# The last 64 rows of q and k loaded four tokens to a partition, batch 1 by SyncE's queue, channel weights issued sooner, the second gather's copies planned later

## The chip, the cores and the metric

The kernel runs on one core of a Trainium2 chip. The metric is the time of one execution on the device in microseconds (us). The engines go by the profile's names: PE is TensorE's matmul and PEld its weight load, DVE is VectorE, ACT is ScalarE, POOL is GpSimd, SP is SyncE. SP and ACT issue loads on hardware queues, POOL on a software queue.

## The reference

For 8 batches of 8 heads, 576 tokens and 64 values a head: attention in which a token sees the 32 tokens to either side, and 8 global tokens see and are seen by all. The result, heads side by side, is the input x (8 x 576 x 512) of a mixer block: one pair of matmuls over tokens, one over channels, each with a residual.

```python
mask = np.abs(pos[:, None] - pos[None, :]) <= window      # window = 32
mask = mask | is_global[:, None] | is_global[None, :]
scores = np.where(mask, scale * (q @ kT), -1e9)
attn = softmax(scores) @ v
...
h = np.maximum(xt @ w_tok1, 0.0) @ w_tok2                 # 576 -> 256 -> 576
u = x + h.transpose(0, 2, 1)
h2 = np.maximum(u @ w_ch1, 0.0) @ w_ch2                   # 512 -> 1536 -> 512
return u + h2
```

The eight global positions are an input, so which columns are global is known only on the chip.

## The kernel before

**Tiles.** All tiles are allotted once. A batch's q and k come as f32 into `lq` and `lk` (128 partitions, 8 heads, four tokens side by side in a partition, 64 values): `load_qk` (L504) thus loads the first 512 tokens in runs of 1 KB. The last 64 rows (`S - LAST` to `S`) of q and of k go into the two halves of one tile, `lr` (L60): `load_rest` (L513) puts one token into a partition, so a run is 64 values, 256 bytes. v goes by tokens into `lv` (`load_v`, L521). `cast_qk` and `cast_v` copy them to f16 (`qk`, `rn`, `vsh`). There is one copy of `lq`, `lk`, `lr`, `lv`, `qk` and `rn`: a batch's load waits for the casts of the batch before.

**Turning.** q and k are needed with the 64 values on the partitions. For batches 0 to 2 PE turns them (`turn_pe` L562, `rest_pe` L583, which turns `rn`), and copies bring them into `qT` and `kT`; from batch 3 on DMA transposes on SP do it (`turn_dma` L639). The copies undo the order of four tokens to a partition.

**Global columns.** For batch 0 `glob_pe` (L594) picks the global tokens out of `qk` and `rn` by matmuls with a one-hot right-hand side `ohq` (L359, made in `f_ohq` L378): for each pair of heads and for q and k, four products for the first 512 tokens and one for the last 64. For the other batches indirect DMAs (`f_gather` L486, on POOL) fetch the rows, the first gather for batches 1 to 3, the second for 4 to 7; `glob_rows` (L616) copies them to f16 (L619) and PE turns them (L623).

**The rest of a batch.** `scores` (L660: matmuls L675, exponential on ACT L685, mask on DVE L691), `glob_keys` (L698), `glob_sums` (L717, matmul L722), `values` (L733, matmuls L742 and L755, division L782 and L783), `token1` (L799), `token2` (L817), `turn_u` (L842), `chan1` (L864, matmul L868, 128x512 each), `chan2` (L889, matmul L911) and the store (L922). In the first 34 us PE also runs matmuls on zeros into free banks (`warm`, L284; their tile is `zt`).

**Order.** The kernel schedules itself when it is built. Every piece of work is entered by `op` (L96) with the engines that may do it and a cost on each, a priority, what it reads and writes, and for a DMA the tuple `dma`: transfer time, weight of its queue against others, time to landing, and number of pieces. `run` (L119) then simulates the engines and the queues, and at each step gives out the piece that could start first; so each engine gets a fixed order of instructions. On the chip an engine works through its order and waits where something is not there yet. `late` adds to the time at which the planner takes a transfer as landed, as does `LATE` (L116) after 36 us. `behind` lets a piece be issued only after another one on the queue. `slot` (L168) gives out the eight banks of PSUM.

**Queues.** For batch 0 SP issues `lr`, `lq`, `lk` and `lv` (L941 to L945). POOL fills constants (`f_pads`, `f_pads2`), then a `gate` (L934, a copy of one column of a tile that a load fills) makes it wait for batch 0's second piece of v, and behind that it issues `w1`, `w1l`, `w2`, the first gather's k half, batch 1's `lr`, `lq` and `lk`, the three thirds of the first channel weights (`f_wc1`, L475) and of the second (`f_wc2`, L481), batch 1's v and batch 2's loads. Loads of batch 3 and later are issued by SP (q, k, rest) and ACT (v), paced by `paced` (L914).

## Time and profile before

| What | Value |
|---|---|
| median of 3 runs | 307.86 us (306.68 to 311.13) |
| profiled execution, device time | 308.4 us |
| its span, first to last instruction | 306.7 us |
| busy, PE / PEld | 289.9 us (95%) / 154.9 us (51%) |
| busy, DVE / ACT / POOL | 187.3 us (61%) / 178.9 us (58%) / 60.2 us (20%) |
| instructions | 7290, of them 2955 matmuls |
| mean granted clock of TensorE | 0.987 |
| moved by DMA | 51.31 MB in 94820 packets, 73730 of them under 512 bytes |

A row of the order of time reads: start, duration, engine (with a q: its queue issuing), line, operation, output <- inputs, shapes, count, and in brackets how long the engine had stood idle and for whom. In a table by stretches each engine has its busy time and its number of instructions, then come the granted clock, the busy share of the DMA engines and GB/s. A row of a group has after the bar its busy time in us and the mean of one in ns. Matmuls overlap: the 128x512 matmul of the first channel stage takes 380 ns by its own row, and eight of them behind one another take 1.89 us.

### The profile page before, as it was taken

The numbers are of one execution on the slowest core, as the hardware profiler recorded it, in microseconds if no ns is written. First come the engines' busy times: TensorE is split into PE (matmuls) and PEld (weight loads), VectorE is DVE, ScalarE is ACT, GpSimd is POOL, SyncE is SP. The second block draws the span as 40 slices with busy tenths as digits, with TensorE's granted clock in tenths as the row PEclk, the third lists the DMA queues.
The fourth block names the chain that finished last, engine by engine and source line by source line (L and its number), as shares of the span: only waits on it lengthen the run. The fifth ranks groups of instructions, "written<-read, shape, count | busy, mean of one in ns | idle before, by whom it ended". The sixth has DMA issues, their size and how long they took to land. (4 is left out here: it accounts for less than half of the span.)

```text
span 306.7 us, 7290 instructions
## 1 busy us (share of the span) xinstructions
PE 289.9 (95%) x2955; PEld 154.9 (51%) x2955; DVE 187.3 (61%) x411; ACT 178.9 (58%) x325; POOL 60.2 (20%) x109
## 2 busy tenths in 40 slices
PE   5969989997999989999989999999999999999995
PEld 3746645444474444544456445444555445444643
DVE  7778866668786536994476655976587357230012
ACT  3873895376986369812996089714992183305600
POOL 8489635642001010002000100002000200020000
PEclk9798999999999999999999999999999999999999
DMA  6988999999997973499946995699844411071013
GB/s 170 257 137 272 220 226 212 298 214 301 193 149 139 309 205 62 96 163 230 311 76 131 218 338 143 98 214 220 288 100 90 135 38 37 8 148 69 0 71 104
DMA packets 94820, 51.31 MB, mean 167 GB/s; under 512 B 73730, under 2 KB 90242, under 8 KB 94786
## 3 DMA queue, kind: packets, MB, share of 16 engines
q1 hardware_dynamic: 62480, 26.36, 39.9%
q0 software_dynamic: 8704, 18.45, 24.1%
q10 hardware_dynamic: 23602, 6.03, 11.1%
q8 instruction: 23, 0.38, 0.5%
q14 instruction: 11, 0.09, 0.1%
HBM read 36.11 MB, written 9.44 MB: 149 GB/s over the span
## 5 line engine op out<-in xcount | busy, mean ns | idle before, releaser
L868 PE MATMUL bank<-uT,wc 128*128 128x512 f16 x384 | 92.3, 380 | 2.5 <-DVE qT L591 1.7
L911 PE MATMUL bank<-wc,b 128*128 128x512 f16 x384 | 87.5, 379 | 0.0
L685 ACT ACTIVATE e<-bank 128x648 f16<-128x648 f32 x64 | 42.9, 740 | 44.3 <-PE bank L675 43.2
L860 ACT ACTIVATE b<-bank 128x512 f16<-128x512 f32 x87 | 51.6, 620 | 26.3 <-PE bank L868 26.2
L911 PEld LDWEIGHTS <-b 128*128 128x128 f16 x384 | 36.8, 98 | 42.6
L868 PEld LDWEIGHTS <-wc 128*128 128x128 f16 x384 | 35.1, 98 | 43.5 <-issue 4.3
L922 POOL DMA_DIRECT2D out_dram<-osb x28 | 15.6, 556 | 198.6 <-DVE osb L919 198.6
L919 DVE TENSOR_TENSOR osb<-u,bank 128x512 f32<-128x512 f16 x32 | 21.9, 686 | 46.3 <-PE bank L911 46.1
L691 DVE TENSOR_TENSOR e<-e,masku 128x1296 f16<-128x1296 f16 x28 | 23.3, 832 | 20.5 <-ACT e L685 20.1
L548 ACT CAST vsh<-lv 128x512 f16<-128x512 f32 (+3 forms) x44 | 26.6, 621 | 7.5 <-DMA lv<-in_v_dram 7.1
L836 DVE TENSOR_TENSOR u<-x,bank 128x512 f16<-128x512 f16 x30 | 18.7, 682 | 8.1 <-PE bank L823 7.8
L783 DVE TENSOR_TENSOR x<-bank,rr 128x512 f16<-128x512 f32 x32 | 22.1, 692 | 1.1
L823 PE MATMUL bank<-a,w 128*128 128x512 f16 x80 | 19.9, 379 | 0.6 <-DVE a L811 0.4
L675 PEld LDWEIGHTS <-kT 64*128 64x128 f16 x576 | 11.3, 96 | 15.2 <-issue 14.1
L805 PE MATMUL bank<-x,w 128*128 128x512 f16 x64 | 18.7, 379 | 0.0
L536 ACT CAST qk<-lk 128x512 f16<-128x512 f32 x27 | 16.6, 627 | 1.7 <-DMA lk<-in_k_dram 1.7
L742 PE MATMUL bank<-rf,lf 128*64 128x264 f16 x144 | 16.1, 294 | 1.2 <-ACT b L860 0.9
L675 PE MATMUL bank<-qT,kT 64*128 64x72 f16 x576 | 15.6, 196 | 1.2 <-ACT e L685 1.2
L536 ACT CAST qk<-lq 128x512 f16<-128x512 f32 x26 | 15.8, 624 | 1.2 <-DMA lq<-in_q_dram 0.7
L755 PEld LDWEIGHTS <-e 128*64 128x64 f16 x576 | 16.1, 115 | 0.1
L755 PE MATMUL bank<-vsh,e 128*64 128x66 f16 x320 | 15.9, 198 | 0.0
L653 DVE COPY kT<-raw 128x512 f16<-128x512 f16 x20 | 12.0, 599 | 5.2 <-DMA raw<-qk 4.9
(166 smaller groups left out, 333.8 us busy)
## 6 DMA issues: line engine op xcount, KB each, us to landing
out_dram<-osb POOLq DMA_DIRECT2D x28, 256.0 KB, 4.3
lq<-in_q_dram SPq DMA_DIRECT2D x11, 512.0 KB, 7.0
lk<-in_k_dram SPq DMA_DIRECT2D x11, 512.0 KB, 9.2
lv<-in_v_dram ACTq DMA_DIRECT2D x15, 256.0 KB, 5.4
wc<-in_moe_w_ch_dram POOLq DMA_DIRECT2D x6, 512.0 KB, 13.3
lq<-in_q_dram POOLq DMA_DIRECT2D x4, 512.0 KB, 8.5
lk<-in_k_dram POOLq DMA_DIRECT2D x4, 512.0 KB, 9.8
lv<-in_v_dram ACTq DMA_DIRECT2D x10, 192.0 KB, 5.7
```

The source lines that it names most:

```text
L536: COPY[e](out=qk[:, ti, p].rearrange("q i (r d) -> q r i d", r=2), in_=(lq, lk)[ti][:, hs])
L548: COPY[e](out=vsh[i][a:z, c, :, 0:D], in_=lv[a:z, c])
L675: nc.tensor.matmul(ps_tile[keys[z]][:, u // 3, UW * (u % 3) : UW * (u % 3) + UW], lhsT=kT[r, 64 * u : 64 * u + P], rhs=qT[r, u // 2, UW * ...
L685: op([("A", 0.595)], pri + 1, lambda e, par=par: nc.scalar.activation(out=es[i][:, 2 * p + par].rearrange("p (n u) x -> p n u x", n=3), in ...
L691: op([("V", 0.85)], pri + 2, lambda e: nc.vector.tensor_mul(out=e2, in0=e2, in1=masku.unsqueeze(1).to_broadcast([P, 2, NB, UW])), r=["mask ...
L755: nc.tensor.matmul(o[:, VW * hh : VW * hh + VW], lhsT=es[i][:, h, 2 * tau + c, x : x + 64], rhs=vod[i][:, tau, h, :] if c else vsh[i][:, t ...
L783: nc.vector.tensor_tensor(out=xo, in0=pq[:, :, :, 0:D], in1=rr.unsqueeze(3).to_broadcast([P, 2, NP, D]), op=ALU.mult,)
L823: nc.tensor.matmul(ps_tile[key], lhsT=w2[:, ch, P * tau - sh : P * tau - sh + P], rhs=a1[:, ch, :], start=(ch == 0), stop=(ch == 1 and not ...
L860: nc.scalar.activation(out=out, in_=in_, func=AF.Relu)
L868: nc.tensor.matmul(ps_tile[key], lhsT=wc1[:, cc, P * j : P * j + P], rhs=uT[:, cc, :], start=(cc == 0), stop=(cc == 3))
L911: nc.tensor.matmul(ps_tile[key], lhsT=w, rhs=wc2[:, j, :], start=(j == 0), stop=(j == NJ - 1))
L919: nc.vector.tensor_add(out=osb, in0=uls[b // 2 % 2] if last else u16s[i][:, tau], in1=ps_tile[key])
```

## The change

- `lr` is laid out as [128, 2, 256]: four tokens side by side in a partition, 16 partitions to a head, two heads per group of partitions (index r). `load_rest` becomes four loads (q and k, r = 0 and 1) in runs of 1 KB, for batch 0 on ACT's queue (`"K"`) instead of SP's.
- `rn` holds the same in f16 with another order, and the copies after the turn (`rest_pe`, `turn_dma`) undo it.
- `glob_pe` needs four products for the last rows, with a one-hot `ohr` that also picks the pair of heads (`f_ohr`), eight matmuls for each sum instead of five. `ohq` gets eight columns of positions instead of six.
- Batch 1's `lr`, `lq` and `lk` are issued by SP behind batch 0's v, not by POOL.
- On POOL batch 1's constants are filled early, a second gate waits for batch 1's third load of q and k, and behind it come the first channel weights, then the second ones and batch 1's v as before. Batch 2's loads and the second gather stand behind these. Fills of `w1l` and `w2` move to `f_pads2`.
- The second gather's copies (`late` 12.0 instead of 0) are planned later.
- The planner's figures: `LATE` 1.5 instead of 2.0, a far larger weight for POOL's queue (`BIG`), dearer v loads on POOL, a lower weight for stores, the cost of changing the kind of matmul only when it changes from `"n"`, and dearer last pieces of `values`.

```diff
-    lr = const.tile([P, H, D], F32, name="lr")
+    lr = const.tile([P, 2, 4 * D], F32, name="lr")
...
-    RING, LATE = 4096, 2.0
+    RING, LATE = 4096, 1.5
...
-                    if e == "P" and o["mode"] != mode:
+                    if e == "P" and mode == "n" != o["mode"]:
                         c = c + 0.095
...
-    op_i = const.tile([P, NT + 1], I32)
+    op_i = const.tile([P, 8], I32)
     nc.gpsimd.iota(op_i[:, 0:4], pattern=[[1, 4]], base=0, channel_multiplier=4)
-    nc.gpsimd.iota(op_i[:, 4:5], pattern=[[1, 1]], base=S - LAST, channel_multiplier=1)
-    nc.gpsimd.iota(op_i[0:LAST, 5:6], pattern=[[1, 1]], base=S, channel_multiplier=1)
-    nc.gpsimd.iota(op_i[LAST:P, 5:6], pattern=[[1, 1]], base=S - LAST, channel_multiplier=1)
+    nc.gpsimd.iota(op_i[:, 4:8], pattern=[[1, 4]], base=S - LAST, channel_multiplier=0)
...
+    pm64 = const.tile([P, 1], F32)
+    nc.vector.tensor_scalar(out=pm64, in0=pm16, scalar1=4.0, scalar2=None, op0=ALU.mult)
+    nc.vector.tensor_scalar(out=op_f[:, 4:8], in0=op_f[:, 4:8], scalar1=pm64, scalar2=None, op0=ALU.add)
...
+    def f_ohr(e):
+        nc.vector.tensor_tensor(
+            out=ohr, in0=ohq[:, 4:8].unsqueeze(1).to_broadcast([P, 2 * NP, 4, NG]),
+            in1=blk.unsqueeze(2).unsqueeze(3).to_broadcast([P, 2 * NP, 4, NG]), op=ALU.mult,
+        )
...
+    op([("V", 0.35)], -186.5, f_ohr, r=["ohq"], w=["ohr"])
...
-    TURN, STORE = (0.75, 256, 0.35, 544), (0.78, 2048, 0.8, 128)
+    TURN, STORE, BIG = (0.75, 256, 0.35, 544), (0.78, 600, 0.8, 128), 100000
...
     def load_rest(b, pri, opts, after=(), late=0.0, ):
         for t, ten in enumerate((q, k)):
-            def f(e, t=t, ten=ten):
-                ENG[e].dma_start(
-                    out=lr[LAST * t : LAST * t + LAST], in_=ten[b, :, S - LAST : S, :].rearrange("h p d -> p h d")
-                )
+            for r in range(2):
+                def f(e, t=t, r=r, ten=ten):
+                    ENG[e].dma_start(
+                        out=lr[LAST * t : LAST * t + LAST, r],
+                        in_=ten[b, :, S - LAST : S, :].rearrange("(p r) (g i) d -> p r g (i d)", r=2, i=4)[:, r],
+                    )
...
-                COPY[e](out=rn.rearrange("p n (r d) -> p (n r) d", r=2), in_=lr)
+                COPY[e](out=rn.rearrange("p i (r d) -> p r i d", r=2), in_=lr.rearrange("p r (i d) -> p r i d", i=4))
...
-            out=kTs[i][:, :, WIN + 512 : WIN + S], in_=ps_tile[key][:, :, LAST:P]), ps=[key], w=[("kTr", i)])
+            out=kTs[i][:, :, WIN + 512 : WIN + S].rearrange("q p (g i) -> q p g i", i=4),
+            in_=ps_tile[key][:, :, LAST:P].rearrange("q i (p g) -> q p g i", p=NP)), ps=[key], w=[("kTr", i)])
...
-                    for t in range(NT):
+                    for t in range(8):
                         nc.tensor.matmul(
-                            pg[:, ti * n + p - pp.start, :], lhsT=qk[:, ti, p, t] if t < 4 else rn[:, p],
-                            rhs=ohq[:, t if t < 4 else 4 + ti, :], start=(t == 0), stop=(t == NT - 1),
+                            pg[:, ti * n + p - pp.start, :], lhsT=qk[:, ti, p, t] if t < 4 else rn[:, t - 4],
+                            rhs=ohq[:, t, :] if t < 4 else ohr[:, NP * ti + p, t - 4, :], start=(t == 0), stop=(t == 7),
                         )
...
-            load_rest(0, -196, [("S", 0.65)])
+            load_rest(0, -196, [("K", 0.5)])
...
-            if b == 1:
-                pl = -173.9
-            load_rest(b, pl, [("G", 0.73)], [n0] if b == 1 else ())
+            load_rest(b, pl if b > 1 else -179, [("G", 0.73) if b > 1 else ("S", 0.6)], [n0] if b > 1 else ())
...
-                    load_qk(b, ti, slice(h, h + 4), pl + 1 + h / 2 if b > 1 else pl + 0.1 + h / 100, [("G", 0.88)], [n0] if b == 1 else ())
+                    load_qk(b, ti, slice(h, h + 4), pl + 1 + h / 2 if b > 1 else -178 + h / 100, [("G", 0.88) if b > 1 else ("S", 0.9)], [n0] if b > 1 else ())
+            if b == 1:
+                gate(-173.5, [("l", 0, 2)], [lq[:, 4, 0, 0:1]])
...
-            op([("G", 0.77)], -173, f_wc1(0), w=[("wc1", 0)], dma=(2.6, 4096, 2.0, 512), behind=[n0])
-            op([("G", 1.0)], -174.5, f_w2, w=["w2"], dma=(2.4, 4096, 2.0, 512), behind=[n0])
-            for t in (1, 2):
-                op([("G", 0.77)], -173 + t, f_wc1(t), w=[("wc1", t)], dma=(2.6, 4096, 2.0, 512), behind=[n0])
+            op([("G", 0.9)], -174.5, f_w2, w=["w2"], dma=(2.4, BIG, 2.0, 512), behind=[n0])
...
-            op([("G", 1.2)], -18, lambda e: qk_pads(1, nc.gpsimd), w=[("qT", 1, p) for p in range(NP)] + [("kT", 1, p) for p in range(NP)] + [("qTr", 1), ("kTr", 1)], behind=[n1])
+            op([("G", 1.2)], -173.9, lambda e: qk_pads(1, nc.gpsimd), w=[("qT", 1, p) for p in range(NP)] + [("kT", 1, p) for p in range(NP)] + [("qTr", 1), ("kTr", 1)], behind=[n2])
...
-                op([("G", 2.7)], (-115 if ti == 0 else -174.2) if b == 0 else 70, f_gather(b, ti), r=["idx"], w=[("g32", b, ti)], dma=(0.1, 256, 1.7, 256), late=0.0 if b or ti else 2.3,
-                   behind=[] if b == 0 and ti == 0 else [n2])
+                op([("G", 2.7)], (-115 if ti == 0 else -174.2) if b == 0 else 70, f_gather(b, ti), r=["idx"], w=[("g32", b, ti)], dma=(0.1, 128, 1.7, 256), late=12.0 if b else (0.0 if ti else 2.3),
+                   behind=[nw] if b else [n2] if ti else [])
...
-            loads(1, n0)
-            op([("G", 0.77)], -40, f_wc2(0), w=[("wc2", 0)], dma=(2.6, 4096, 2.0, 512), behind=[len(ops) - 1])
+            loads(1)
+            n0 = len(ops) - 1
+            for t in range(3):
+                op([("G", 0.77)], -173 + t, f_wc1(t), w=[("wc1", t)], dma=(2.6, BIG, 2.0, 512), behind=[n0])
+            op([("G", 0.77)], -40, f_wc2(0), w=[("wc2", 0)], dma=(2.6, BIG, 2.0, 512), behind=[len(ops) - 1])
...
+            nw = len(ops) - 1
```

53 lines of the change are left out of this document (29 added, 24 removed).

## The prediction

> **What bounds the kernel now.** I read the head of the page first, then the busy time by stretches, then the warm-up matmuls alone (they read and write nothing that counts), then the order of time around each idle stretch of PE.
>
> ```profile
> span 306.7 us, 7290 instructions
> ```
>
> ```profile
> core 0: us, PE busy (x) PEld busy (x) DVE busy (x) ACT busy (x) POOL busy (x), PEclk, DMA share, GB/s
> 0.00:7.00 7.00, 3.61 (x16) 2.03 (x16) 5.24 (x33) 2.15 (x4) 5.82 (x27) 1.00 0.59 161
> 7.00:22.00 15.00, 12.31 (x213) 8.55 (x215) 11.22 (x37) 13.01 (x25) 9.95 (x18) 0.89 1.07 208
> 22.00:35.00 13.00, 12.49 (x168) 9.14 (x165) 11.54 (x29) 6.37 (x13) 11.60 (x18) 0.87 0.94 244
> 35.00:60.00 25.00, 23.42 (x280) 12.03 (x278) 16.82 (x34) 16.85 (x31) 13.91 (x19) 1.00 1.14 241
> ...
> 69.00:76.00 7.00, 5.09 (x65) 3.33 (x63) 5.84 (x11) 4.42 (x10) 1.71 (x3) 1.00 1.50 320
> 76.00:300.00 224.00, 221.33 (x2153) 113.37 (x2153) 130.02 (x258) 129.43 (x235) 13.27 (x24) 1.00 0.66 147
> 300.00:306.70 6.70, 2.94 (x26) 2.28 (x24) 1.53 (x3) 0.00 (x0) 0.00 (x0) 0.90 0.37 119
> ```
>
> ```profile
> 0.00:7.00 7.00, 3.56 (x15) 1.93 (x15) 0.27 (x1) 0.21 (x1) 1.00 0.59 161
> 7.00:22.00 15.00, 2.39 (x13) 1.14 (x13) 0.00 (x0) 0.00 (x0) 0.89 1.07 208
> 22.00:35.00 13.00, 1.20 (x8) 0.74 (x8) 0.00 (x0) 0.00 (x0) 0.87 0.94 244
> ```
>
> The reader is to see that TensorE (PE) sets the time, and that only the first quarter has something to give. From 76 to 300 us PE is idle for 2.67 of 224 us. Before that it is idle for 3.39, 2.69, 0.51, 1.58 and 1.91 us in the five stretches shown, 10.1 us in all, and 7.15 us of its busy time up to 35 us are warm-ups (3.56, 2.39, 1.20). So about 17 us before 76 us hold no work. The end (300 to 306.7) is not touched by the change. The profiled execution took 308.4 us, 1.7 more than its span; the median of the runs is 307.86. I make the sum against 308.4, which stands 0.2% above that median.
>
> **Part 1, the start: the last rows leave SyncE's queue.**
>
> ```profile
> 0.82 0.77 SPq L516 DMA_DIRECT2D lr<-in_q_dram  x1
> 1.25 0.52 ACTq L445 DMA_DIRECT2D gidx_r<-in_global_idx_dram  x1
> 2.30 0.62 SPq L506 DMA_DIRECT2D lq<-in_q_dram  x1
> 6.34 0.62 ACT L533 CAST rn<-lr 128x512 f16<-128x512 f32 x1 [4.03 <-DMA lr<-in_k_dram]
> 6.87 0.61 ACT L536 CAST qk<-lq 128x512 f16<-128x512 f32 x1
> ```
>
> SP issues two `lr` loads first, so batch 0's first `lq` goes out at 2.30. The change puts `lr` behind the index load on ScalarE's queue, and `lq` can go at 0.82, 1.48 us sooner; its cast at 6.87 was behind the `rn` cast, which waited for `lr` until 6.34. The four new issues cost 4 x 0.52 = 2.1 us on ACT after 1.77, under its 4.03 us wait. Bounds: a gain of 1.5 if all follows `lq`, a loss of 0.5 if `rn` comes later (its last issue at 1.77 + 3 x 0.52 = 3.3 instead of 0.82 + 0.77 = 1.6, some of it made good by smaller and fewer pieces) and ACT takes it first. I take a gain of 1.0, nearer to `lq`.
>
> **Part 2, three more matmuls for each global sum.** A position's column now needs four products for the last rows instead of one: 8 sums x 3 = 24 matmuls. Nothing in the trace has the new right-hand side; the nearest rows:
>
> ```profile
> 9.07 0.29 PE L601 MATMUL bank<-ohq,qk 128*128 128x8 f16 x4
> L408 DVE TENSOR_TENSOR masku<-band,rowh 128x256 f16<-128x256 f16 x1 | 0.4, 417 | 0.0
> L656 DVE COPY qT<-raw 128x512 f16<-128x512 f16 x20 | 11.7, 600 | 0.5 <-DMA raw<-qk 0.3
> L648 DVE COPY qT<-rawr 128x256 f16<-128x256 f16 x5 | 1.1, 225 | 0.7 <-DMA rawr<-rn 0.7
> ```
>
> Four take 0.29 us, at most 0.07 each, so 24 take up to 1.7 us, all inside 7 to 22 us, where PE has 2.69 us idle and 2.39 us of warm-ups as cover. The new one-hot (`f_ohr`, 256 elements: 0.42 us) and two small vector operations go into DVE's chain ahead of the first scores. Bounds 0 and 1.7 lost; I take 0.2, since ACT (13.01 of 15 us) and not PE paces that stretch. The copies of the turned last rows become strided: 600 ns for 512 elements strided (L656) is 300 for 256, against 225 (L648), so some 75 ns in 10 copies, 0.8 us of DVE, and DVE is idle 94 of the 224 us there: nothing. From batch 1 on a batch has four `lr` issues instead of two, two more at about 0.62 us (the row at 2.30); they run a batch ahead of their use, so nothing again, and 1.2 us a batch if that lead were gone.
>
> **Part 3, batch 1's q and k go by SyncE's queue, and the channel weights move up in POOL's.**
>
> ```profile
> 17.00:23.00 6.00, 4.22 (x104) 2.78 (x105) 4.57 (x14) 4.29 (x9) 5.39 (x8) 0.92 0.89 123
> 6.00:9.00 3.00, 1.72 (x19) 1.47 (x20) 2.63 (x11) 2.66 (x6) 2.44 (x7) 0.90 0.93 292
> ```
>
> ```profile
> 6.28 8.74 SPq L525 DMA_DIRECT2D lv<-in_v_dram  x5
> 23.09 0.84 POOL L506 DMA_DIRECT2D lq<-in_q_dram  x1
> 28.54 0.60 ACT L809 ACTIVATE a<-bank 128x512 f16<-128x512 f32 x1 [2.48 <-PE bank L805]
> 31.00 0.42 DVE L536 CAST qk<-lk 128x512 f16<-128x512 f32 x1
> 33.24 1.06 PE L568 MATMUL bank<-ident,qk 128*128 128x128 f16 x16
> 33.82 0.60 ACT L852 COPY uT<-bank 128x512 f16<-128x512 f16 x1
> 34.48 1.05 PE L568 MATMUL bank<-ident,qk 128*128 128x128 f16 x16
> 35.37 1.89 PE L868 MATMUL bank<-uT,wc 128*128 128x512 f16 x8
> ```
>
> Now SP is done at 15.0 and stands still, while POOL issues batch 1's q and k from 23.09. After the change they stand behind batch 0's v on SP, at about 14. By then 17 to 23 us moves only 123 GB/s, against 292 in 6 to 9, so batch 1's q and k (2 x 8 x 576 x 64 x 4 bytes, 2.4 MB) fit in some 8 us: I estimate the third load, for which the new gate on POOL waits, landed at 23 to 26 us. What that buys: ACT, which sits 2.48 us idle before 28.54, can cast batch 1 there; DVE loses casts like the one at 31.00 out of the chain that makes `u`; and the 32 transposes (33.24 and 34.48, 2.1 us) no longer stand between the last `uT` copy, done at 34.42, and the first channel matmul at 35.37. I take 0.95 for that gap and 1.15 for two to three casts fewer in the chain ahead: 2.1. Bounds: 0 if ACT's room comes at the wrong time, 3.3 if the transposes and the warm-ups of that stretch (2.1 + 1.2) all go.
>
> That needs the weights too:
>
> ```profile
> L476 POOL DMA_DIRECT2D wc<-in_moe_w_ch_dram x1: 829/829/829, 26.1 to 26.1; - x1
> ...
> DMA to landing us min/median/max: 8.9/8.9/8.9
> ```
>
> ```profile
> 49.68 0.62 ACT L548 CAST vsh<-lv 96x512 f16<-96x512 f32 x1 [0.67 <-DMA lv<-in_v_dram]
> 50.35 0.24 PE L722 MATMUL bank<-vsh,eg 128*32 128x132 f16 x4 [0.25 <-ACT vsh L548]
> ```
>
> The first third of the channel weights is issued at 26.1 and lands at 35.0, 0.4 before its first use: today no earlier start was possible. In the changed order it is issued behind the gate, at 24 to 27, but the 2.4 MB ahead of it in POOL's queue are gone, so I expect it at 29 to 31. Batch 1's v comes behind it; its last piece holds PE at 50.35 today. Of the 1.58 us that PE idles in 35 to 60, I take 0.9 as gained (bounds 0 and 1.6). Everything on POOL waits behind the gate: all channel weights, batch 1's v, batch 2's loads and the second gather. Batch 1's fills of constants are moved ahead of it, into the time that POOL waits anyway.
>
> By the Trainium skill ("DMA: Bandwidth & Descriptors", section "Issuing engines are not separate DMA queues") loads issued from different engines share the same 16 DMA engines, and another issuer saves only its issue time. By that alone this part would be worth nothing; its result is rival 2, and the 123 GB/s speak against it.
>
> **Part 4, the second gather's copies.**
>
> ```profile
> 69.73 0.23 DVE L619 CAST g_q<-g_q 128x128 f16<-128x128 f32 x1 [2.16 <-DMA g_q<-in_q_dram,idx_i]
> 71.85 0.30 ACT L619 CAST g_k<-g_k 128x128 f16<-128x128 f32 x1 [2.33 <-DMA g_k<-in_k_dram,idx_i]
> 73.34 1.02 PE L868 MATMUL bank<-uT,wc 128*128 128x512 f16 x4 [1.73 <-DVE qT L591]
> L623 PE MATMUL bank<-ident,g_q x2: 219/219/219, 26.3 to 130.1; 128*128 128x128 f16 x2
> ```
>
> DVE and ACT each stand over 2 us in front of a gather that the planner thought landed; the copies that free PE's bank are queued behind, and PE idles 1.73 us. The second gather's result is used first at 130.1. Planned 12 us later, the copies wait for nothing. Next late is batch 2's own data. I take 1.6 (bounds 0 and 1.9, all the idle time from 69 to 76).
>
> **Part 5, the planner's other figures** (landing margins, POOL's share, the cost of changing kind of matmul) do no work; they reorder. In 76 to 300 that can win at most part of 2.67 us; bounds a gain of 1.0 and a loss of 1.5; I take 0.
>
> **Sum.** 1.0 - 0.2 + 2.1 + 0.9 + 1.6 = 5.4; 308.4 - 5.4 = **303.0 us**. Its own range, by about half of each bound, is 300.5 to 306.
>
> **The rivals.** *1, more than the sum:* two stretches before 35 us run at a lower granted clock: 0.89 over 15 us and 0.87 over 13 us, 1.65 + 1.69 = 3.3 us of clock not granted. If batch 1's work fills the holes, the second stretch need not come, and if Part 3 also reaches 3.3 and the start 1.5: 303.0 - 1.7 - 1.2 - 0.5 = 299.6. For it: eight warm-ups in that stretch are there to be replaced. Against: the values of batch 0 stay a chain of short steps. The Trainium skill ("TensorE: Matmul & The Clock Gate", Part 1) says that an idle window of about 3.4 us brings half clock, on a window that runs free of the kernel; where it falls is then partly chance, and no single trace here shows that. Chance 0.26.
>
> *2, the transfers are hidden anyway:* the DMA engines are shared, and batch 1 comes no sooner than now, because w1, w2 and the gathers take the room from 17 to 23. Then Part 3 falls away, and 1.0 - 0.2 + 1.6 = 2.4 remain: 306.0. For it: DMA share 0.89 in that stretch. Against: 123 GB/s beside it. Chance 0.19.
>
> *3, slower:* the gate on POOL. It waits for a load that stands behind batch 0's v and behind the last casts of batch 0's q and k (one buffer). The first channel weights then land about 5 us after it opens (0.83 to issue, and about 4.6 by the `lq` load that was issued at 2.30 and cast at 6.87). The point where it decides is 30 us: later than that, they land after today's 35.0, and PE has little else. If it opens at 36, they land at 41, and PE loses 6 us there, gives back 1 of it, and keeps Part 4 and the start: 308.4 + 5 - 2.4 = 311.0. Against: it needs a delay of 10 us over my estimate. Chance 0.06.
>
> *4, the change does not do what it says in Part 4:* later planning only shifts the wait to another transfer, such as batch 2's v; 1.6 falls away, 304.6. Chance 0.07, inside the forecast's own range. The forecast itself: 0.42.
>
> **How the numbers follow.** Two per cent, about what a measurement of this kernel tells from no change, is 301.7 and 314.0 beside the median. Faster by over 2%: rival 1 nearly whole (0.25) and the lower end of the forecast (0.13), 0.38. Slower by over 2%: the upper part of rival 3 and reorderings that I can't price, 0.04. The rest, 0.58, is within. The range runs from 298.8, under rival 1, to 308.6, above rival 2 and without rival 3; some 0.2 lies outside.
>
> **What would show it.** Right: the first `lq` cast before 6.3; batch 1's q and k casts on ACT before 28.5; the first channel matmul at 33 or sooner, with its weights landed by 31; no gather wait over 0.5 us on DVE or ACT near 70; PE idle under 0.6 us in the 7 us around the place of 69 to 76; PE idle under 1 us in the 25 us after the first channel matmul. Wrong: the first channel matmul waiting for a weight load (rival 3), batch 1's casts still after 28.5 (rival 2), or PE idle over 4 us between 76 and 300, which would mean that the new order costs what the start gains.

## The result

The changed kernel takes 319.87 us (median of 6 runs; the kernel before 309.49 beside it): the ratio is 1.0324, with a 95% interval of 1.0253 to 1.0394. It is 3.2% slower where 303.0 us was forecast. (Ratios leave out executions over 1.5% above the fastest of their kernel, among them one of 1021 us here and nine of the twelve of e12.) The profiled execution took 320.87 us.

The head of its page and its busy time by stretches, with the columns as before:

```profile
span 319.2 us, 7365 instructions
```

```profile
core 0: us, PE busy (x) PEld busy (x) DVE busy (x) ACT busy (x) POOL busy (x), PEclk, DMA share, GB/s
7.00:22.00 15.00, 9.34 (x152) 7.01 (x150) 7.87 (x29) 6.96 (x13) 9.33 (x19) 1.00 0.92 183
22.00:35.00 13.00, 10.99 (x212) 7.52 (x209) 12.15 (x35) 8.82 (x18) 6.58 (x13) 1.00 0.96 230
35.00:60.00 25.00, 24.38 (x299) 12.85 (x298) 18.96 (x42) 19.54 (x37) 12.98 (x18) 1.00 1.15 239
...
69.00:76.00 7.00, 6.94 (x62) 4.20 (x61) 5.29 (x10) 4.38 (x10) 1.70 (x3) 1.00 1.47 299
...
100.00:120.00 20.00, 13.75 (x110) 6.52 (x109) 9.29 (x16) 7.82 (x13) 2.32 (x4) 0.93 0.78 217
...
76.00:300.00 224.00, 213.47 (x2089) 108.20 (x2088) 141.70 (x278) 122.08 (x218) 13.81 (x25) 0.98 0.67 146
```

PE idles 5.66 us from 7 to 22 (2.69 before). From 35 to 60 and from 69 to 76 it idles 0.62 and 0.06 us, where before it idled 1.58 and 1.91: the forecast gains are there. From 76 to 300 it idles 10.53 us in place of 2.67, and 6.25 of these lie between 100 and 120, where the change moves nothing by intent. The 0.93 and 0.98 in the last two rows come from one stretch: from 117.17 to 124.00 the granted clock is 0.50.

**The start**, from the order of time of all engines:

```profile
0.82 0.46 SPq L516 DMA_DIRECT2D lq<-in_q_dram  x1
3.63 1.26 ACTq L527 DMA_DIRECT2D lr<-in_k_dram  x2
5.07 0.65 DVE L548 CAST qk<-lq 128x512 f16<-128x512 f32 x1
5.46 0.16 PE L459 MATMUL bank<-gidx_h,ones 1*128 1x8 f16 x1 [1.88 <-DVE gidx_h L458]
7.02 1.06 PE L580 MATMUL bank<-ident,qk 128*128 128x128 f16 x8
12.47 0.62 ACT L545 CAST rn<-lr 128x512 f16<-128x512 f32 x1 [6.92 <-DMA lr<-in_k_dram]
13.14 0.61 PE L599 MATMUL bank<-ident,rn 128*128 128x128 f16 x4 [5.06 <-ACT rn L545]
```

`lq` is cast at 5.07 (6.87 before), as forecast. But the last rows, 256 KB in all and issued by 4.9, are cast at 12.47 where the old ones were at 6.34, and PE stands 5.06 us for them.

The clock column needs care here. It reads 1.00 where the profile has no record, and the first record of this trace is at 18.19. The eight turning matmuls at 7.02 take 1.06 us, as long as sixteen of the same at 33.24 before: PE's steps are at half rate as far as its rows go before 18.19 (106 to 107 ns for 128 columns, up to 15.4), and at full rate from 19.3 on (55 to 56 ns).

**The stretch from 100 to 120**, ACT with its queue and then PE:

```profile
101.91 4.62 ACTq L537 DMA_DIRECT2D lv<-in_v_dram  x3
106.57 0.58 ACT L868 COPY uT<-bank 128x512 f16<-128x512 f16 x1 [3.70 <-PE bank L866]
106.65 4.09 ACTq L537 DMA_DIRECT2D lv<-in_v_dram  x1
110.83 0.58 ACT L868 COPY uT<-bank 128x512 f16<-128x512 f16 x1 [3.68 <-issue]
110.94 3.40 ACTq L537 DMA_DIRECT2D lv<-in_v_dram  x1
114.38 2.40 ACT L560 CAST vsh<-lv 32x512 f16<-32x512 f32 x4 [2.47 <-issue]
117.76 1.30 ACT L701 ACTIVATE e<-bank 128x648 f16<-128x648 f32 x2
111.96 0.26 PE L691 MATMUL bank<-qT,kT 64*128 64x72 f16 x5 [1.49 <-ACT uT L868]
118.51 0.70 PE L691 MATMUL bank<-qT,kT 64*128 64x72 f16 x17 [4.76 <-ACT e L701]
```

The reader is to see what stands between the `uT` copies: ACT issues five loads of v (of batch 4), and one issue takes up to 4.1 us. The copy at 106.57 is put down to PE's bank, but that bank was written by 104.7; it is the issue ahead of it that ended at 106.53. PE waits twice, 6.25 us in all: 1.49 us for a bank that a `uT` copy empties, then 4.76 us for one that an exponential empties. That exponential, at 117.76, stands on ACT behind the last issue, which ends at 114.34, and behind casts of v. The wait has a second price: the matmuls begun until 124.00, at a granted clock of 0.50, take some 2.8 us more than at full rate (an estimate from the column cost given below).

**Parts 3 and 4**, in the order of time of POOL, ACT and DVE:

```profile
27.39 0.76 DVE L548 CAST qk<-lq 128x512 f16<-128x512 f32 x2
28.89 0.62 ACT L548 CAST qk<-lk 128x512 f16<-128x512 f32 x1 [0.99 <-DMA lk<-in_k_dram]
30.40 0.18 POOL L953 COPY hold<-lq 128x1 f32<-128x1 f32 x1 [6.26 <-DMA lq<-in_q_dram]
30.63 2.33 POOL L486 DMA_DIRECT2D wc<-in_moe_w_ch_dram  x3
42.09 1.02 PE L886 MATMUL bank<-uT,wc 128*128 128x512 f16 x4 [0.24 <-ACT uT L868]
79.50 0.69 DVE L937 TENSOR_TENSOR osb<-u,bank 128x512 f32<-128x512 f16 x1 [1.22 <-DMA out_dram<-osb]
```

The new gate opens at 30.40, not at 23 to 26. Batch 1's casts of q and k begin on DVE at 27.39, 1.6 us sooner than before (29.03), and end at 36.92, 2.0 us later (34.94). The weights are issued 4.5 us later than before. They are not waited for: the late start and two groups of batch 1's scores ahead of it have moved the first channel matmul to 42.09 (35.37 before), where it waits 0.24 us for a `uT` copy. The gather's copy at 86.99 waits for nothing.

### The profile page after: what moved, and what is told of

It is laid out like the page before. It is cut to its first block, busy times and chain, and to the rows that moved or that the text cites. A ratio compares the mean times of both kernels' runs of the same rounds, so it can differ in the third digit from the quotient of the medians.

```text
span 319.2 us, 7365 instructions
## 1 busy us (share of the span) xinstructions
PE 293.2 (92%) x2979; PEld 155.7 (49%) x2979; DVE 200.0 (63%) x433; ACT 171.3 (54%) x306; POOL 55.9 (18%) x104
## 3 DMA queue, kind: packets, MB, share of 16 engines
q10 hardware_dynamic: 23874, 6.29, 10.9%
## 4 chain that ended last, share of the span: by engine, by line
issue 46%; PE 31%; DVE 7%; DMA 6%; POOL 5%; ACT 3%; SPq 0%; POOLq 0%; DVEq 0%; ACTq 0%
PE bank L886 12%; PE bank L929 9%; POOL out_dram L940 3%; DMA lr<-in_k_dram 3%; DMA out_dram<-osb 2%; PE bank L691 1%; PE bank L839 1%; DVE x L799 1%; PE bank L580 1%; DVE vod L568 1%; DMA lk<-in_k_dram 1%; PE bank L758 1%; PE bank L898 1%; PE bank L916 1%; DVE qT L583 1%
## 5 line engine op out<-in xcount | busy, mean ns | idle before, releaser
L886 PE MATMUL bank<-uT,wc 128*128 128x512 f16 x384 | 93.7, 385 | 2.4 <-DVE osb L937 1.6
L876 ACT ACTIVATE b<-bank 128x512 f16<-128x512 f32 x75 | 45.1, 604 | 35.7 <-PE bank L886 35.6
L937 DVE TENSOR_TENSOR osb<-u,bank 128x512 f32<-128x512 f16 x32 | 21.9, 687 | 48.1 <-PE bank L929 43.0
L560 ACT CAST vsh<-lv 128x512 f16<-128x512 f32 (+3 forms) x42 | 25.4, 625 | 11.0 <-DMA lv<-in_v_dram 8.2
L691 PE MATMUL bank<-qT,kT 64*128 64x72 f16 x576 | 17.1, 201 | 8.6 <-ACT e L701 5.1
L852 DVE TENSOR_TENSOR u<-x,bank 128x512 f16<-128x512 f16 x30 | 18.7, 682 | 8.2 <-PE bank L839 6.7
L691 PEld LDWEIGHTS <-kT 64*128 64x128 f16 x576 | 12.3, 99 | 23.1 <-issue 22.5
L878 DVE TENSOR_SCALAR b<-bank 128x512 f16<-128x512 f32 x21 | 14.5, 690 | 6.4 <-PE bank L886 6.1
L568 DVE COPY vod<-vsh 64x2112 f16<-64x2112 f16 (+1 forms) x18 | 11.6, 644 | 10.4 <-ACT vsh L560 9.9
L771 PE MATMUL bank<-vsh,e 128*64 128x66 f16 x320 | 15.1, 194 | 0.2 <-DVE x L799 0.2
L771 PEld LDWEIGHTS <-e 128*64 128x64 f16 x576 | 15.0, 111 | 0.4 <-issue 0.2
```

The costliest lines, as they stand in the source:

```text
L560: COPY[e](out=vsh[i][a:z, c, :, 0:D], in_=lv[a:z, c])
L691: nc.tensor.matmul(ps_tile[keys[z]][:, u // 3, UW * (u % 3) : UW * (u % 3) + UW], lhsT=kT[r, 64 * u : 64 * u + P], rhs=qT[r, u // 2, UW * ...
L771: nc.tensor.matmul(o[:, VW * hh : VW * hh + VW], lhsT=es[i][:, h, 2 * tau + c, x : x + 64], rhs=vod[i][:, tau, h, :] if c else vsh[i][:, t ...
L876: nc.scalar.activation(out=out, in_=in_, func=AF.Relu)
L886: nc.tensor.matmul(ps_tile[key], lhsT=wc1[:, cc, P * j : P * j + P], rhs=uT[:, cc, :], start=(cc == 0), stop=(cc == 3))
```

## The experiments

Eighteen kernels ran. Beside the times I use a second measure, **lost time**. Steps inside dense rows give 0.42 ns a column (216 ns for 512), and half or a quarter of that for matmuls that use 64 or 32 rows or columns of PE. The 8-column products step by 25 to 27 ns, so narrow ones count as some 60 columns, and each matmul has about 2 ns on top. With these I add up the matmuls begun in a stretch, warm-ups at nothing, and call the rest of the stretch lost; half clock thus counts as lost too. It is worked out, to some tenths of a us. e3 below, which has the order and the loads of before, loses 17.6, 7.3, 1.3, 2.0 and 8.9: differences under 1 us, and under 2 us in the last column, say little.

| lost us in | span | to 35 | 35–80 | 80–100 | 100–120 | 120–300 |
|---|---|---|---|---|---|---|
| before | 306.7 | 18.3 | 6.9 | 1.3 | 2.2 | 6.9 |
| changed | 319.2 | 21.9 | 5.1 | 1.6 | 7.7 | 10.9 |
| e1 16 engines | 312.4 | 21.6 | 3.9 | 0.7 | 7.1 | 7.2 |
| e5 parts 1, 2 | 321.7 | 22.5 | 5.6 | 4.2 | 6.6 | 10.9 |
| e6 parts 3, 4 | 312.7 | 19.9 | 6.4 | 2.0 | 1.8 | 11.5 |
| e7 part 5 | 314.6 | 17.7 | 8.2 | 0.9 | 7.5 | 9.1 |
| e8 parts 3, 4, 5 | 311.8 | 19.3 | 6.8 | 0.8 | 2.4 | 11.5 |
| e13 LATE alone | 315.3 | 17.3 | 7.4 | 0.8 | 8.0 | 10.6 |
| e14 parts 3, 4, behind | 312.3 | 18.7 | 5.3 | 0.6 | 6.7 | 9.7 |
| e15 parts 1 to 4 | 315.9 | 21.6 | 6.3 | 7.4 | 0.3 | 8.4 |
| e16 same, 16 engines | 308.6 | 20.4 | 6.7 | 0.7 | 2.0 | 6.9 |
| e17 e13, v behind | 306.9 | 18.2 | 8.9 | 0.9 | 0.8 | 7.2 |
| e18 e1, v behind | 305.2 | 21.6 | 3.9 | 0.9 | 0.8 | 6.1 |

### The last rows' loads: 4 or 16 DMA engines

The busy time of the DMA queues between 4 and 12 us (packets, MB, share); first the changed kernel, then e1. q10 is ACT's queue.

```profile
q10 hardware_dynamic: 272, 0.26, 12.1%
```

```profile
q10 hardware_dynamic: 320, 0.26, 12.0%
```

The four loads are 256 runs of 1 KB, so 16 packets are left in the one and 64 in the other: 4 or 16 a load. The Trainium skill ("DMA: Bandwidth & Descriptors", section "Why a DMA increments its semaphore by 16 and not by 1") gives the rule: a load uses the largest number of engines up to 16 that divides the slowest dimension of both sides, and each engine used posts once. The trace agrees: the new load's source has four pairs of heads outermost, and 4 posts a load.

**e1** puts head pairs inside and the 16 groups of four tokens outside; seven small DVE operations for the one-hot go with it. **e2** does it for batch 0 only. Both otherwise are the changed kernel.

```diff
-  in_=ten[b, :, S - LAST : S, :].rearrange("(p r) (g i) d -> p r g (i d)", r=2, i=4)[:, r],
+  in_=ten[b, :, S - LAST : S, :].rearrange("(p r) (g i) d -> g p r (i d)", r=2, i=4)[:, :, r],
```

> The changed kernel with another order of the last rows inside lr (partition 4g+p instead of 16p+g), so that the source of each of the four loads begins with a dimension of 16 instead of 4; the order of instructions on all engines stays that of the changed kernel, but for seven small DVE operations. Theory A (each new lr load runs on only four of the 16 DMA engines, since 4 semaphore writes per load are seen instead of 16, and holds up what shares those four): 16 semaphore writes per load, the 256 packets of batch 0 are through in 2 us instead of 8, the rn cast waits for lr under 2 us instead of 6.9, the ACT-issued lv loads near 105 us take under 2 us each, and the time falls by 8 to 14 us to 305 to 312. Rival B (the new order of the instructions is worse by itself, through the planner's changed figures): the packets may spread, but the time stays within 3 us of the changed kernel, 316 to 322. Rival C (ScalarE's queue is slow for such loads whatever their shape): rn still waits over 5 us and the time stays above 315.

> The same edit for batch 0 alone: batches 1 to 7 keep the loads whose source begins with a dimension of 4. It parts the loss at the start from the loss later. Theory A: the rn wait at the start goes (under 2 us), some 4 to 5 us are gained against the changed kernel, and the lv loads issued by ACT near 105 us still stall it for 3 us or more, so 314 to 317. If the start alone is the cause: as fast as the first kernel of this set. Rival B: no change, 316 to 322.

Measured: e1 315.23 us, ratio to before 1.0183 (1.01 to 1.0266); e2 316.96, 1.021 (1.0143 to 1.0277). e1's start, ACT and PE:

```profile
10.22 0.62 ACT L549 CAST rn<-lr 128x512 f16<-128x512 f32 x1 [4.71 <-DMA lr<-in_k_dram]
10.90 0.61 PE L603 MATMUL bank<-ident,rn 128*128 128x128 f16 x4 [2.81 <-ACT rn L549]
```

Spreading the loads takes 4.6 us off the whole, with the order of PE, ACT, POOL and SP in the trace as in the changed kernel. That is less than theory A's 8 to 14 us. The rows come 2.25 us sooner, but up to 35 us that wins next to nothing (21.6 lost instead of 21.9). Most comes late (120 to 300 loses 7.2 instead of 10.9), and part of that is the clock: the half clock of the changed kernel's stall reaches into this column (117.17 to 124.00), that of e1 does not (110.84 to 114.26). 10.22 is still not the 6.34 of before, and the stall from 100 to 120 stays. e2's ratio can't be told from e1's, so the pair does not part batch 0 from the later ones.

**e3** was to make the kernel before use four engines, by splitting its source dimension.

```diff
-  in_=ten[b, :, S - LAST : S, :].rearrange("h p d -> p h d")
+  in_=ten[b, :, S - LAST : S, :].rearrange("h (a p) d -> a p h d", a=4)
```

> The kernel before, its order of instructions untouched, with the 64 rows of each lr load split in the source into 4 times 16, so that its slowest dimension is 4. Theory A: each lr load then runs on four DMA engines, its 512 packets of 256 bytes queue there, rn waits 4 to 8 us longer at the start, and the kernel before becomes 4 to 10 us slower, 312 to 318. Rivals B and C: nothing changes, 306 to 311.

Measured: 308.95, 0.9971 (0.994 to 1.0003). The trace still has 16 posts a load: the edit did nothing (that the split dimension is merged again is likely, not shown). It tells nothing of engines and serves as a repeat of before.

**e11** is e1 with batch 0's last rows issued first on SP (`("K", 0.5)` becomes `("S", 0.6)`), as before the change.

> The changed kernel with the 16-engine layout in all batches, and batch 0's four lr loads issued by SP ahead of q and k, as the kernel before has its two. Theory A, for the start: lr issued on ACT lands behind the q and k that SP issued before it, so here rn is cast before 7.5 us instead of 10 to 12, PE's wait for rn falls under 2 us, and the idle time up to 35 us falls by 2 to 4 us against the 16-engine kernel: 311 to 314. Rival: SP's four issues of 0.5 us each delay q and k as much as rn gains, 314 to 317.

Measured: 316.67, 1.0239 (1.0165 to 1.0314), and 21.9 us lost up to 35, as much as in e1. Now `rn` is cast at 5.27, but its products at 10.46 wait for `ohr` on DVE, and the index matmul still runs at 5.45 (3.52 before). The time is the rival's (314 to 317): the rows are in time, and the start is no shorter. The first `lq` now goes out at 3.46 instead of 0.82 and its cast is at 7.74, and `ohr` stands on DVE behind the small operations that e1 added. Queue and order changed together here, so which of them made the rows late in e1 is not shown.

### The change taken apart

**e5**: the kernel before with parts 1 and 2 alone (layout, `glob_pe`, batch 0's rows on ACT's queue). **e6**: with parts 3 and 4 alone. **e7**: with part 5 alone. **e8**: the changed kernel with the old layout, so parts 3, 4 and 5. **e4**: the kernel before with the one figure of part 4:

```diff
-  late=0.0 if b or ti else 2.3,
+  late=12.0 if b else (0.0 if ti else 2.3),
```

> The kernel before with parts 1 and 2 alone: the last rows four tokens to a partition, four loads, for batch 0 on ACT's queue, eight matmuls for each global sum; queues of batch 1, the channel weights, the gathers and the planner's figures as before. Theory A (the loss is in these loads: at the start they land behind batch 0's q and k, later they run on four engines): most of the loss is here, the rn cast waits over 5 us at the start, and the time is 313 to 320. Rival B (the planner's figures make a worse order): 307 to 311.

> The kernel before with parts 3 and 4 alone: batch 1's q, k and last rows by SP, the channel weights behind the new gate, batch 1's constants early, the second gather behind the weights and planned 12 us later; the old layout and the old figures. Prediction, parts 3 and 4: 2.1 + 0.9 + 1.6 us gained, 303 to 306. Rival 2 of the prediction (transfers hidden anyway): 307 to 309. Rival 3 (the gate): over 310.

> The kernel before with part 5 alone: the planner's figures (LATE 1.5, the weight of POOL's queue, dearer v loads on POOL, a lower weight of stores, the cost of changing the kind of matmul, dearer last pieces of values); every transfer and every computation as before, only the order differs. Theory A: within 3 us of the kernel before, 307 to 312. Rival B: the order alone costs most of the loss, 314 to 320, with the stall of ACT by its own v loads near 105 us.

> The changed kernel without parts 1 and 2: the old layout, one token to a partition in two loads, for batch 0 on SP ahead of q and k; all the rest of the change in it. Theory A: the loss goes and the gains of parts 3 and 4 show, 302 to 306. Rival B: it stays slow, 312 to 320, and the stall of PE between 100 and 120 us stays over 4 us.

> The kernel before with the second gather planned to land 12 us later, nothing else: only the two copies of its result move in DVE's and ACT's order. The prediction's fourth part: the waits of 2.16 and 2.33 us go, PE's 1.73 us idle near 73 us goes, and the time falls by 1 to 1.9 us. Rival: the idle time is only moved to the next wait, and the time stays within 0.5 us.

Measured: e5 323.36, 1.0399 (1.0271 to 1.0527); e6 314.24, 1.0127 (1.0019 to 1.0234); e7 314.01, 1.0161 (1.0087 to 1.0235); e8 314.75, 1.0155 (1.0024 to 1.0287); e4 309.7, 0.9997 (0.9966 to 1.0029). e6 and e8 miss what parts 3 and 4 promised (303 to 306, and 302 to 306). Every large part is slower by itself, and the three do not add up (13 + 4 + 4 against 10 us in all), so something is shared. The table shows what: the loss at 100 to 120 is there in e5, e7, the changed kernel and e1, and not in e6 and e8. e5 has the old figures, so such an order can come without the new ones too. In e4 the gather's wait goes (70 to 75 loses 1.2 instead of 2.4) and comes back at once (75 to 80 loses 1.5 instead of 0.5).

In e6 the loss is where the gate and v are. From its order of time:

```profile
21.42 0.45 DVE L549 CAST vsh<-lv 96x512 f16<-96x512 f32 x1 [1.86 <-DMA lv<-in_v_dram]
22.44 0.46 PE L723 MATMUL bank<-vsh,eg 128*32 128x132 f16 x17 [2.30 <-DVE eg L695]
27.73 0.18 POOL L936 COPY hold<-lq 128x1 f32<-128x1 f32 x1 [4.07 <-DMA lq<-in_q_dram]
```

Batch 0's last v comes at 21.4 (cast at 18.69 before), and PE stands 2.30 us. SP issues batch 1's `lr` ahead of the last two pieces of v. **e14** therefore holds batch 1's loads on SP behind batch 0's last v (their `behind` becomes that load; parts 3 and 4 otherwise).

> The kernel before with parts 3 and 4, and batch 1's q, k and last rows held on SP until batch 0's last piece of v has been issued. Its written order also puts two uT copies behind the loads of v of batch 4, so 100 to 120 us may cost as in the kernel with part 5 alone; the comparison is made up to 60 us. Theory (what parts 3 and 4 alone lose at 20 to 25 us is batch 0's v, delayed by batch 1's loads that go ahead of its last pieces): PE has lost 17 us or less at 35 us, against 18.3 before and 19.9 with parts 3 and 4 alone, and the VectorE copy of v that was at 18.7 before and at 21.4 there is back before 19.5. Rival (the transfers share the DMA engines whatever the order of issue): still 19 or more lost at 35 us. Time 310 to 315 in both.

Measured: 316.18, 1.0218 (1.0157 to 1.0278), above the 310 to 315 expected. v is cast at 18.88 again, and 18.7 us are lost at 35 instead of 19.9, but that is neither under the 17 of the theory nor the 19 of the rival: the new order has PE wait 2.98 us at 22.21 for batch 1's `rn` cast instead. So v's delay was part of the loss; the queue alone is not the gain either. The rest of its time is the stall at 100 to 120.

### The order of ACT

**e9** and **e10** tried whether the kernel before is only a lucky order: one planner figure each (exponential 0.62 instead of 0.595; the time between engines 0.1 instead of 0.06) gives another order without touching anything else.

> The kernel before, with one planner figure that the change does not touch: the exponential on ACT planned at 0.62 instead of 0.595 us. No transfer, tile or computation differs; some 1500 lines of PE's order of 5900 and 400 of ACT's move. Theory D (the kernel before has a lucky order, and any other order of this planner costs 3 to 6 us on the chip, since the planner sees ACT's own DMA issues and late transfers too kindly): 312 to 316. Theory E (the order is not delicate, and the changed figures and queues each cost by their own effect): 308 to 311, as the kernel before.

> The kernel before with another planner figure that the change does not touch: 0.10 instead of 0.06 us from one engine to the next. Some 1100 lines of PE's order and 160 of ACT's move. Theory D: 312 to 316. Theory E: 308 to 311.

Measured: 310.17, 0.9991 (0.9953 to 1.0029), and 309.73, 0.9972 (0.993 to 1.0015). These two orders are not slower; the theory that any other order is falls.

What is particular is where ACT issues batch 4's v. Before, its order has three of ACT's four `uT` copies of batch 2, a load, the fourth copy, and four loads:

```profile
103.52 0.59 ACT L852 COPY uT<-bank 128x512 f16<-128x512 f16 x1 [0.93 <-PE bank L850]
103.58 6.01 ACTq L525 DMA_DIRECT2D lv<-in_v_dram  x4
```

The issues are long there too (the third of these four takes 3.70 us), but no copy stands behind them. The changed kernel (DVE has one of the copies) has three loads, a copy, a load, two copies, the last load. In e6, e15 and e16, which have no stall, all four copies come first, in e8 two, a load, and two. **e12** takes the loads off ACT (e1 with v of batches 3 to 7 issued by POOL: `("A", 0.6)` becomes `("G", 0.87)`).

> The 16-engine kernel with v of batch 3 and later issued by POOL instead of ACT. Theory F (the stall of PE between 100 and 120 us is ACT held for 4 to 8 us by its own v issues, with PE's evacuations queued behind): ACT's waits that end in no releaser go, PE is idle under 2 us from 100 to 120 instead of 4.6, and the time falls by 3 to 6 us to 309 to 312. Rival: the DMA engines are full there in any case and the stall only moves, 313 to 317.

Measured: 1.0036 (0.9977 to 1.0094), from three runs of 310.93 to 312.06; the other nine took 315.79 to 320.63. The profiled run (315.87) is one of the nine: about 1 us is lost at 100 to 120, and about 14 behind that. So the stall there is gone, but the rival, that it only moves, is not excluded by this run.

**e13** is the kernel before with LATE 1.5 instead of 2.0 and nothing else. This puts four of the five loads ahead of all four copies.

```diff
-    RING, LATE = 4096, 2.0
+    RING, LATE = 4096, 1.5
```

> The kernel before with one planner figure alone, the landing margin LATE 1.5 instead of 2.0; nothing else differs. Its written order puts all four late loads of v of batch 4 ahead of the last three uT copies on ACT (before: three copies first). Theory (that order is the cause of the stall at 100 to 120 us, whichever edit brings it): PE loses 6 us or more at 100 to 120 against 2.2 before, and the time is 313 to 316. Rival (the figures cost only as a set): 309 to 311, and the stretch loses under 4 us.

Measured: 318.94, 1.0309 (1.0212 to 1.0407). One figure that does no work costs 9 us. ACT and PE there:

```profile
99.93 9.24 ACTq L525 DMA_DIRECT2D lv<-in_v_dram  x2
109.26 0.59 ACT L852 COPY uT<-bank 128x512 f16<-128x512 f16 x1 [10.14 <-DMA lv<-in_v_dram]
110.94 2.72 PE L911 MATMUL bank<-wc,b 128*128 128x512 f16 x6 [5.94 <-ACT uT L852]
```

These are the third and the fourth of the row; they occupy ACT for 9.24 us (5.12 and 4.03), where the two ahead of them, from 98.16 on, took 0.34 and 1.24. The copy behind them waits 10.14, PE 5.94, and the granted clock is 0.50 from 107.06 to 113.89. **e17** moves only those loads: e13 with batch 4's v entered behind the four copies.

```diff
-            load_v(b, pl + 6, [("A", 0.6)], n0)
+            load_v(b, pl + 6, [("A", 0.6)], [ucopy[2, t] for t in range(4)] if b == 4 else n0)
```

> The kernel with LATE 1.5 alone (318.94 us, PE loses 8.0 us at 100 to 120), and batch 4's loads of v entered on ACT behind the four uT copies of batch 2. Theory (the loads of v, standing ahead of those copies in ACT's order, are the cause): the stretch from 100 to 120 loses 2 to 3 us and the time is 309 to 312. Rival (the loads of batch 4 come into the way of something there wherever they stand, for example of the casts that need them): the loss moves to 120 to 140 and the time stays above 315.

Measured: 309.5, 0.9991 (0.9959 to 1.0023). The 9 us are gone, with all but six of PE's 2955 matmuls in the order of e13. Its ACT, where the loads now follow:

```profile
105.88 0.59 ACT L854 COPY uT<-bank 128x512 f16<-128x512 f16 x1 [0.93 <-PE bank L852]
106.32 0.34 ACTq L525 DMA_DIRECT2D lv<-in_v_dram  x1
106.69 0.55 ACTq L525 DMA_DIRECT2D lv<-in_v_dram  x1
118.05 2.38 ACTq L525 DMA_DIRECT2D lv<-in_v_dram  x3
```

Two loads go out from 106.32 on, in 0.34 and 0.55 us, and three at 118.05. So the cause of the stall is shown: the place of these loads in ACT's order, ahead of the copies. Why a load behind two or three others takes up to 5.1 us to issue was not parted: q, k and rows of the batch are moving on SP's queue then, and loads of v stand ahead on ACT's own.

### Both together

**e15** is the changed kernel without part 5, whose order happens to have the copies first; **e16** the same with 16 engines.

> The changed kernel without part 5 (the planner's old figures): parts 1 to 4. Its written order has four uT copies ahead of all loads of v of batch 4. Theory (4 against 16 DMA engines costs at the start, the order costs at 100 to 120): no stall at 100 to 120 (lost under 3 us), 21 to 22 us lost at 35 us as in the changed kernel, in all 313 to 316. Rival (the layout itself brings the stall, since the loads of the last rows hold the queues): 6 us or more lost at 100 to 120 and 318 to 321.

> The same with the last rows placed so that each load's slowest dimension is 16, which spreads it over all 16 DMA engines; four uT copies ahead of the loads of v here too. Theory: 19 to 20 us lost at 35 us, 2 less than with 4 engines, no stall at 100 to 120, and 310 to 313. Rival (the number of engines does not matter): within 1 us of the run with 4 engines beside it.

Measured: e15 318.28, 1.03 (1.0226 to 1.0373); e16 310.67, 1.0049 (1.001 to 1.0088). The stall at 100 to 120 is in neither. But e15 was expected at 313 to 316, and loses 7.4 us at 80 to 100, in a place that no theory named. Its POOL, DVE and PE:

```profile
73.34 1.14 POOL L938 DMA_DIRECT2D out_dram<-osb  x2 [0.86 <-DVE osb L935]
83.07 0.69 DVE L935 TENSOR_TENSOR osb<-u,bank 128x512 f32<-128x512 f16 x1 [5.14 <-DMA out_dram<-osb]
83.81 0.94 PE L691 MATMUL bank<-qT,kT 64*128 64x72 f16 x17 [4.29 <-DVE osb L935]
```

The result's buffer comes free only when a store has landed, DVE waits 5.14 us for that, and PE 4.29. Again the clock follows: it is 0.50 from 83.11 to 89.94, which makes up the rest of the 7.4. With 16 engines this is gone (0.7), and the two orders are nearly the same on all engines. So the pair shows that the narrow loads cost this; by which way they make the store late (the four engines, or the later issues) it does not.

**e18** is the changed kernel with both mends: e1's line and e17's.

> The changed kernel with both mends: the last rows spread over 16 DMA engines (315.23 us by itself), and batch 4's loads of v behind the uT copies of batch 2. Theory (these two are what the change lost, and its gains at 35 to 76 us stay): 100 to 120 loses 2 to 3 us in place of 7.1, and the time is 309 to 311, no better than before, because up to 35 us about 2 to 3 us more are lost than before. Rival (the other planner figures cost by themselves): 313 or more, with the loss spread over 120 to 240.

Measured: 306.75 us, 0.9882 (0.9857 to 0.9907) against 309.97 before: 1.2% faster, the best of all, and better than I expected. Its stretches:

```profile
7.00:22.00 15.00, 10.97 (x158) 7.59 (x155) 10.17 (x37) 8.71 (x17) 10.91 (x23) 1.00 1.06 202
22.00:35.00 13.00, 11.45 (x202) 7.53 (x201) 12.09 (x37) 8.27 (x17) 7.27 (x12) 0.87 0.97 236
35.00:60.00 25.00, 24.62 (x300) 13.13 (x301) 19.03 (x40) 18.85 (x36) 12.53 (x17) 1.00 1.13 249
...
100.00:120.00 20.00, 20.00 (x193) 9.46 (x191) 12.92 (x25) 13.87 (x26) 1.62 (x3) 1.00 1.18 245
...
76.00:300.00 224.00, 223.36 (x2173) 114.94 (x2171) 144.35 (x281) 122.92 (x219) 13.81 (x25) 1.00 0.65 146
```

It still loses 3.3 us more than before up to 35, wins 3.0 back between 35 and 80, and 2.6 after that (80 to 300 loses 7.8 against 10.4). So the two causes explain the loss: from 319.87 to 315.23 by the engines, to 306.75 by the order. PE's order in the trace is the same in all three. The new figures, but for the place of these loads, are still in e18: the expectation's rival, that they cost by themselves, falls.

## Why the prediction was wrong

**Part 5 failed, and it was the dearest.** It said that the figures "do no work; they reorder", with a loss of 1.5 at most and 0 taken. One of them alone costs 9 us (e13), and in the changed kernel 8.5 (e1 to e18). The bound was taken from PE's idle time before, 2.67 us; that limits what a new order can win, not what it can lose. What a move can lose is read at the engine that does the moved work: ACT's issues of v are among its instructions. "PE idle over 4 us between 76 and 300" was named as a sign that the new order costs what the start gains. It came. The figures are one way to such an order, not the only one: e5 has it with the old ones.

**Part 1 failed in the sign.** The step "a loss of 0.5 if `rn` comes later", with "some of it made good by smaller and fewer pieces", is the wrong one: `rn` is cast 6.1 us later (12.47 for 6.34), not the 1.7 that the prediction has for its last issue. +1.0 was forecast, with −0.5 as the lower bound; up to 35 us the new layout loses 3.6 us more than before with all parts, 4.2 with parts 1 and 2 alone. The step on `lq` was right (5.07, 1.8 us sooner); but `lq` did not pace. 1 KB pieces on a quarter of the engines explain a part of the delay: 16 engines bring `rn` from 12.47 to 10.22. Its issue ahead of q and k on SP's queue brings it to 5.27 (e11). Neither makes the start shorter, so the rows are not all that holds it; what else does stays open, with one candidate under part 2.

**Part 2** was right on PE: rows of the changed start have a group of four `ohr` products every 0.10 us, so 24 more cost 0.6 us of PE, under its bound. It was wrong to take DVE's chain at 0.2: the index matmul moves from 3.52 to 5.46, and PE stands 1.88 us for it between its warm-ups. In all nine traces with this matmul at 5.4 to 5.5 the half rate of the start lasts to the first record of the clock, at 14.3 to 20.7 us; in the eleven with it at 3.52, to 4.4 to 10.8. No run moved that matmul alone, so this is a link and not a shown cause. "Four `lr` issues instead of two… nothing again" failed as well, by way of the number of engines: e15 to e16 is 7.6 us, most of it the one wait for a store and the half clock behind it.

**Part 3**: two steps failed. The estimate "the third load landed at 23 to 26" is the first; measured are 27.73 (e6), 28.12 (e18) and 30.40. 123 GB/s before showed room in the stretch, but SP also had batch 0's v to bring, and batch 1's rows went ahead of it. The second is what sooner casts were to buy. In e6 batch 1's first four casts of q and k lie between 23.05 and 27.38 (before, from 29.03 on), and yet the first channel matmul comes at 38.43, in e18 at 41.27, where it was at 35.37. So the 2.1 did not come, and e6 lost 1.6 us more up to 35 instead. The later half, 0.9 between 35 and 60, came: PE idles 0.62 there, 0.43 in e6 and 0.38 in e18, against 1.58. Rival 2 (batch 1 comes no sooner) is not what e6 shows, and only roughly what the changed kernel does. Rival 3 had its gate open after 30 us, but not its price: no matmul waited for a weight, because PE came to its channel matmuls only at 42.09.

**Part 4**: alone it is worth nothing, the wait moves 5 us on (e4), as rival 4 said. Together with the others the 1.9 us from 69 to 76 are won (0.06 idle), of which 75 to 80 takes back 1.4 (1.9 lost instead of 0.5) in a wait for a store. That this is part 4's work is not shown: with parts 1 and 2 alone (e5) PE idles 0.00 us from 69 to 76, with parts 3 and 4 alone (e6) 2.19.

**Rival 1**'s clock: the 1.00 that the column gives the changed kernel from 7 to 22 is no gain, since PE's steps there are at half rate until the first record at 18.19. Matmuls begun at half rate up to 35 us cost some 3.1 us more than at full rate, 3.4 before and 4.3 in e18 (estimates from the column cost). So the clock neither gave what rival 1 hoped nor makes the difference up to 35. Behind 35 us it counts: some 2.8 us in the changed kernel, none before and in e18. The prediction's condition for half clock, an idle window of about 3.4 us, is more than these traces need: before, the clock is 0.50 from 8.42 on, and PE's longest wait in the 3.4 us ahead of that is 2.13 us.

In sum, both large losses come from terms taken as nothing: part 5, and the number of engines that a load runs on. Behind 35 us e18 wins 3.0 and 2.6. Part 3's 0.9 is among this; the rest can't be put down to parts 3 and 4, since with the old layout they win only 0.5 (e6) and 0.1 (e8) between 35 and 80, and the 2.6 behind 80 was not forecast at all.

## What to carry to other kernels

When a load's shape changes, look at its outermost dimension before its run length: fewer, longer runs on a quarter of the engines were slower, and reordering the same dimensions recovered 4.6 us. A DMA issue is an instruction in its engine's order: when a planner's figures change, list which loads moved ahead of which copies, and treat a load ahead of a copy that PE needs as a risk of the whole issue time (up to 5.1 us here), not of its nominal half microsecond. Count the half clock that can follow a long wait of PE, and read a clock of 1.00 at the start of a trace beside the steps of equal matmuls. The idle time before bounds a gain from reordering and bounds no loss.

## What was not expected of the hardware

- An issue on ACT's queue takes 0.34 us as the first of a row and up to 5.1 us behind others (two in 9.24), and a copy behind it waits that long (10.14 us in e13).
- In the runs of the table, each wait of PE over 4 us behind 35 us has a stretch at a granted clock of 0.50 beginning in it, 3.4 or 6.8 us long: 4.76 us in the changed kernel, 5.42 in e5, 5.94 in e13, 4.54 in e14, 4.29 in e15.
- One small DVE operation of the index chain (128x8, at 3.20 to 3.39) takes 1.61 us in the changed kernel and 1.42 in e16, where it took 0.28 before; what holds it was not tried and stays open.
- Another issuer alone did not bring the last rows sooner: by ACT from 1.8 on, with SP's first loads ahead of them, and on 16 engines, they are cast at 10.22 (e1); by SP as its first loads, at 5.27 (e11).
